# One load per side for a 576-row weight: 96 partitions of six rows instead of 128 partitions of four and a tail

## The chip, the cores and the metric

The kernel runs on one core of a Trainium2 chip. The metric is device time in microseconds (us) of one execution. The kernel before was timed in three runs: 249.95, 250.19 and 251.74 us, median 250.19 us. One execution was profiled; all durations below are from it.

## The reference, cut to what matters

Two independent decode steps of attention, A and B, each with one query token, 32 query heads, 16 key/value heads and a head size of 128. A attends to the last 2048 positions of its cache, B to all 8192. Everything is bf16.

```python
q = (x @ wq)                      # x: 1 x 576, wq: 576 x 4096  -> 32 heads of 128
k, v = k_cache[:, :, -W:], v_cache[:, :, -W:]   # W = 2048 (A), 8192 (B); 16 heads, each used twice
p = softmax(q @ k.T * 128**-0.5)
out = concat_heads(p @ v) @ wo    # wo: 4096 x 576
return concat([out_A, out_B])     # 1 x 1152
```

What has to be read from memory is wq and wo of both sides (4.72 MB each, four of them) and the caches (8 pairs of heads, each with 4.19 MB of B keys, 1.05 MB of A keys and the same of values).

## The kernel before, in words

**The ring.** All large loads go into one SBUF tensor, `ring`, of 73,728 bf16 elements on each of 128 partitions. `place` (L167) hands out consecutive stretches of it, starts again at 0 when a stretch doesn't fit, and makes the load wait for the last use of whatever its stretch overlaps. All loads are issued on SP in the order in which they are placed: wq of A, wq of B, then for each of 8 head pairs p the B keys, A keys, B values, A values, then wo of A in one piece and wo of B in six pieces. A load that waits holds up all loads behind it on SP. The two rows of x come over ACT's queue.

**wq before.** Of the 576 rows, 512 are loaded as 128 partitions of four rows (L197, 4.19 MB), the other 64 as 128 half rows (L199, 0.52 MB). In the ring, wq of A holds elements 0 to 18432, wq of B 18432 to 36864, the first keys and values follow, and the first B values (up to 73728) end exactly at the ring's end, so that the first seven loads wait for nothing.

**Spreading x.** The query is computed so that each of 128 output rows holds the same q: the stationary operand is a column of x repeated 128 times. `xT` (L272) makes these by five matmuls of a strided piece of x against ones; the fifth takes each of the last 64 elements twice, which `xd` (L263, VectorE) has written into `xdup` first. `xr` (L275, L278, VectorE) copies the results from PSUM to `xrep`; the fifth block is copied twice, each time multiplied by a 0/1 column `par` (L247) that keeps the even or the odd partitions, since an odd partition holds the second half of its row.

**q.** `qmm` (L295) makes q in eight pieces of 512 columns per side, five accumulating matmuls each. It waits for wq of its side and for all `xr` of both sides. ACT and VectorE take turns in evicting (`qe`), VectorE transposes (`qT`, L306) and scatters q into the zeroed stationary operands `zb` and `za` (`z0`, `z1`).

**The pairs.** For each head pair, VectorE transposes ten slabs of keys (`T`, L335), TensorE makes scores from each (`S`, L345), the maximum, the exponential and its transposes follow, and TensorE multiplies by the values (`V`, L393 and L400). `F` (L457) is the product with wo at the end, and two stores write the output. GpSimd builds identity and ones and clears `zb`, `za`, `pts` at the start (L229 to L241).

Of the kernel before, what the change touches and what calls it, by code (L numbers as in the profile page):

```python
# [4 lines left out]
BF16 = mybir.dt.bfloat16  # L5
F32 = mybir.dt.float32
I32 = mybir.dt.int32
ALU = mybir.AluOpType
ACT = mybir.ActivationFunctionType
AX = mybir.AxisListType  # L10
# [4 lines left out]
DM = 576  # L15
# [5 lines left out]
SLAB = 2048  # L21
NB = 2 * SK // 128 * DH // SLAB
NI = NB + 2
W0 = 2 * (NB - 1)
ZW = 128 + W0
RING = 72 * 1024
# [5 lines left out]
class Prog:  # L32
# [9 lines left out]
    def op(self, eng, fn, deps=(), name=None):  # L42
        self.ops[eng].append((fn, tuple(deps), name, None))
        if name is not None:
            assert name not in self.where, name
            self.where[name] = (eng, len(self.ops[eng]) - 1)
# [60 lines left out]
def bass_concat_heads__sliding_block_cached__gqa_block_cached__decode_kernel(nc, A_x, A_k_cache, A_v_cache, A_wq, A_wo,  # L107
                         B_x, B_k_cache, B_v_cache, B_wq, B_wo, out):
    xs, ks, vs = [A_x, B_x], [A_k_cache, B_k_cache], [A_v_cache, B_v_cache]
    wqs, wos = [A_wq, B_wq], [A_wo, B_wo]  # L110
# [7 lines left out]
    identf = nc.alloc_sbuf_tensor("identf", [128, 128], F32)  # L118
    onesf = nc.alloc_sbuf_tensor("onesf", [128, 128], F32)
    onesb = nc.alloc_sbuf_tensor("onesb", [1, 128], BF16)  # L120
    xrow = nc.alloc_sbuf_tensor("xrow", [1, 2 * DM], BF16)
    xdup = nc.alloc_sbuf_tensor("xdup", [1, 2, 128], BF16)
    xrep = nc.alloc_sbuf_tensor("xrep", [128, 2, 6, 128], BF16)
    qsb = nc.alloc_sbuf_tensor("qsb", [128, 2, 512], BF16)

# [10 lines left out]
    cls = nc.alloc_sbuf_tensor("cls", [128, 8], F32)  # L136
    selb = nc.alloc_sbuf_tensor("selb", [128, 16], F32)
    sela = nc.alloc_sbuf_tensor("sela", [128, 4], F32)
    par = nc.alloc_sbuf_tensor("par", [128, 2], F32)
    lsel = nc.alloc_sbuf_tensor("lsel", [128, NP, 8], F32)  # L140
    rl = nc.alloc_sbuf_tensor("rl", [128, NP * 8], F32)
    xo = nc.alloc_sbuf_tensor("xo", [128, 2, 512], F32)
# [12 lines left out]
    def view(t, free, offset, dims, parts=128, p0=0):  # L155
        return bass.AP(tensor=t, offset=p0 * free + offset, ap=[[free, parts], *dims])

    pg = Prog(nc)
    op, load = pg.op, pg.load
# [7 lines left out]
    def place(size, uses, issue, name):  # L167
        if at[0] + size > RING:
            at[0] = 0
        lo, hi = at[0], at[0] + size  # L170
        at[0] = hi
        deps = []
        for r in list(live):
            if r[0] < hi and lo < r[1]:
                deps += r[2]
                live.remove(r)
        n = nload[0]
        nload[0] += 1
        if n >= NSEM:
            deps += uses_of[n - NSEM]  # L180
        uses_of.append(list(uses))
        live.append((lo, hi, list(uses)))
        t = ring[:, lo:hi]
        load("sp", lambda e: issue(e, t), s_ld[n % NSEM], 16 * (n // NSEM + 1), deps=deps, name=name)
        return t

    for P in range(2):
        x = xs[P]
# [4 lines left out]
    wq_at = {}  # L193
    w = HQ * DH
    for P in range(2):
        uses = ["qmm%d.7" % P]
        main = wqs[P][0:512, :].rearrange("(p k) n -> p (k n)", k=4)  # L197
        wq_at[P, 0] = place(4 * w, uses, lambda e, t, main=main: e.dma_start(t, main), "wq%d.0" % P)
        tail = wqs[P][512:DM, :].rearrange("r (c n) -> (r c) n", c=2)  # L199
        wq_at[P, 1] = place(w // 2, uses, lambda e, t, tail=tail: e.dma_start(t, tail), "wq%d.1" % P)  # L200

    kv_at = {}
    for p in range(NP):
        for kind, c in (("K", ks), ("V", vs)):
            use = "T%d.%d" if kind == "K" else "V%d.%d"
            src = c[1][0, 2 * p:2 * p + 2, :, :].rearrange("h (q t) d -> (h q) (t d)", q=64)
            kv_at[kind, p, 0] = place(NB * SLAB, [use % (p, NB - 1)],
                                      lambda e, t, src=src: e.dma_start(t, src), "%sB%d" % (kind, p))
            src = c[0][0, 2 * p:2 * p + 2, SK - W_A:SK, :].rearrange("h (q t) d -> q h (t d)", q=128)
            kv_at[kind, p, 1] = place(2 * SLAB, [use % (p, NI - 1)],  # L210
                                      lambda e, t, src=src: e.dma_start(t.rearrange("q (h n) -> q h n", h=2), src),
# [3 lines left out]
    for P in range(2):  # L215
        k0 = 0
        for c, kk in enumerate(NWO[P]):
            src = wos[P].rearrange("(p k) n -> p (k n)", k=HQ)[:, k0 * DM:(k0 + kk) * DM]
# [4 lines left out]
    def slab(kind, p, s):  # L223
# [9 lines left out]
       deps=["id0"], name="ident")  # L233
# [9 lines left out]
    op("act", lambda e: e.activation(warm[:, 4:8], warm[:, 0:4], ACT.Exp), deps=["warm0"], name="warm1")  # L243
    for b in range(2):
        op("dve", lambda e, b=b: e.memset(vb[b][:, :], 0.0), name="vb0.%d" % b)
    for c in range(2):
        op("dve", lambda e, c=c: e.tensor_reduce(par[:, c:c + 1], view(identf, 128, c, [[2, 64]]), AX.X, ALU.add),  # L247
           deps=["identf"], name="par%d" % c)
    for h in range(2):
        op("dve", lambda e, h=h: e.tensor_reduce(  # L250
            cls[:, 2 * h:2 * h + 2], view(identf, 128, 64 * h, [[1, 2], [32, 2], [2, NB]]), AX.XY, ALU.add),
            deps=["identf"], name="clsB%d" % h)
    op("dve", lambda e: e.tensor_reduce(cls[:, 4:8], view(identf, 128, 2 * NB, [[1, 4], [32, 4]]), AX.X, ALU.add),
       deps=["identf"], name="clsA")
    op("dve", lambda e: e.tensor_reduce(selb[:], view(identf, 128, 0, [[1, 16], [32, 4]]), AX.X, ALU.add),
       deps=["identf"], name="selb")
    op("dve", lambda e: e.tensor_reduce(sela[:], view(identf, 128, 0, [[4, 2], [1, 2], [32, 4], [2, 2]]), AX.XY, ALU.add),
       deps=["identf"], name="sela")


    banks = [sb[0], sb[1], qb[0], qb[1]]
    for P in range(2):
        op("dve", lambda e, P=P: e.tensor_copy(  # L263
            view(xdup, 256, 128 * P, [[2, 64], [1, 2]], parts=1),
            view(xrow, 2 * DM, P * DM + 512, [[1, 64], [0, 2]], parts=1)), deps=["x%d" % P], name="xd%d" % P)
        for k in range(5):
            def mm(e, P=P, k=k):
                if k < 4:
                    lhsT = view(xrow, 2 * DM, P * DM + k, [[4, 128]], parts=1)
                else:  # L270
                    lhsT = xdup[0:1, P, :]
                return e.matmul(banks[2 * P + k // 4][:, (k % 4) * 128:(k % 4 + 1) * 128], lhsT=lhsT,  # L272
                                rhs=onesb[0:1, :], start=True, stop=True)
            op("pe", mm, deps=["x%d" % P, "onesb", "xd%d" % P], name="xT%d.%d" % (P, k))
        op("dve", lambda e, P=P: e.tensor_copy(  # L275
            xrep[:, P, 0:4, :].rearrange("p k m -> p (k m)"), banks[2 * P][:, :]), deps=["xT%d.3" % P], name="xr%d.0" % P)
        for c in range(2):
            op("dve", lambda e, P=P, c=c: e.tensor_scalar(  # L278
                xrep[:, P, 4 + c, :], banks[2 * P + 1][:, 0:128], par[:, c:c + 1], None, ALU.mult),
                deps=["xT%d.4" % P, "par%d" % c], name="xr%d.%d" % (P, 1 + c))  # L280
    XR = ["xr%d.%d" % (P, c) for P in range(2) for c in range(3)]

    KT = NKT * SLAB
    for P in range(2):
        for n in range(8):
            u = 8 * P + n
            bank = banks[u % 4]

            def mm(e, P=P, n=n, bank=bank):
                for k in range(5):  # L290
                    if k < 4:
                        lhsT, o = xrep[:, P, k, :], wq_at[P, 0][:, k * w + n * 512:k * w + (n + 1) * 512]
                    else:
                        lhsT, o = xrep[:, P, 4 + n // 4, :], wq_at[P, 1][:, (n % 4) * 512:(n % 4 + 1) * 512]
                    ins = e.matmul(bank[:, :], lhsT=lhsT, rhs=o, start=(k == 0), stop=(k == 4))  # L295
                return ins
            op("pe", mm, deps=["wq%d.0" % P, "wq%d.1" % P] + XR + (["qe%d" % (u - 4)] if u >= 4 else []),
               name="qmm%d.%d" % (P, n))
            deps = ["qmm%d.%d" % (P, n)] + (["qT%d" % (u - 2)] if u >= 2 else [])
            if n % 2 == 0:  # L300
                op("act", lambda e, n=n, bank=bank: e.activation(qsb[:, n % 2, :], bank[:, :], ACT.Copy),  # L301
                   deps=deps, name="qe%d" % u)
            else:
                op("dve", lambda e, n=n, bank=bank: e.tensor_copy(qsb[:, n % 2, :], bank[:, :]),
                   deps=deps, name="qe%d" % u)
            op("dve", lambda e, n=n: e.transpose(  # L306
                ktb[:, n * 512:(n + 1) * 512].bitcast(I32), qsb[:, n % 2, :].bitcast(I32)),
                deps=["qe%d" % u] + (["z0.%d" % i for i in range(8)] if P else []), name="qT%d" % u)
        srcs = [[512, NP], [64, 2], [1, 2], [128, 2]]
        for b in range(4):  # L310
            if P == 1:
                op("dve", lambda e, b=b: e.tensor_copy(
                    view(zb, NP * 4 * ZW, 32 * b + W0, [[4 * ZW, NP], [2 * ZW, 2], [ZW, 2], [1, 2]], 32, 32 * b),
                    view(ktb, KT, b // 2 * 256, srcs, 32, 32 * b)),
                    deps=["qT%d" % u for u in range(8, 16)] + ["zb0"], name="z1.%d" % b)
            else:
                for h in range(2):
                    op("dve", lambda e, b=b, h=h: e.tensor_copy(
                        view(za, NP * 1024, h * 512 + 32 * b + 2 * (NB + h),
                             [[1024, NP], [256, 2], [128, 2], [1, 2]], 32, 32 * b),  # L320
                        view(ktb, KT, h * 256, srcs, 32, 32 * b)),
                        deps=["qT%d" % u for u in range(8)] + ["za0"], name="z0.%d" % (2 * b + h))
# [6 lines left out]
    for p in range(NP):  # L329
        for s in range(NI):  # L330
            k = p * NI + s
            kt = ktb[:, (k % NKT) * SLAB:(k % NKT + 1) * SLAB]
            deps = [unit("K", p, s)]
            deps += ["S%d" % (k - NKT)] if k >= NKT else Z
            op("dve", lambda e, p=p, s=s, kt=kt: e.transpose(kt.bitcast(I32), slab("K", p, s).bitcast(I32)),  # L335
               deps=deps, name="T%d.%d" % (p, s))
# [12 lines left out]
            deps = ["T%d.%d" % (p, s)]  # L349
# [5 lines left out]
           deps=["S%d" % (p * NI + NI - 1)] + (["mT%d" % (p - 1)] if p else []), name="max%d" % p)  # L355
        op("pe", lambda e: e.matmul(mb[0:1, 0:128], lhsT=mx[:, 0:1], rhs=identf[:, :], start=True, stop=True),  # L356
           deps=["max%d" % p, "identf"] + (["mrA%d" % (p - 1), "mrB1.%d" % (p - 1), "nb%d" % (p - 1)] if p else []),
           name="mT%d" % p)
# [146 lines left out]
```

## Time and profile before

| | us |
|---|---|
| median of three runs | 250.19 |
| the profiled execution | 250.0 |
| its span, first to last instruction | 248.2 |
| TensorE matmul busy | 181.7 (73%) |
| VectorE busy | 153.1 (62%) |
| ScalarE busy | 18.1 |
| GpSimd busy | 13.4 |
| bytes read | 102.76 MB, 414 GB/s over the span |

"Busy" is time in which an engine has an instruction in execution, including one that is held up inside the engine. The time of the profiled execution is 1.8 us over its span: start and end around the instructions. The row of the DMA engines in the page gives the mean busy share of 16 engines in forty slices of 6.2 us; the row below it gives the rate. A load is listed with the time from its issue to the landing of its last byte, which includes the time that it queues behind the loads before it.

### The profile page before, as it was taken

Reading aid. Unit: us, or ns where it says so; the run is one execution under the profiler, and the core shown is the slowest. Engines: PE = TensorE matmul, PEld = TensorE weight load, DVE = VectorE, ACT = ScalarE, POOL = GpSimd, SP = SyncE. Lnnn points to the kernel's source line nnn. Section 1 sums busy time; section 2 is a strip of 40 time slices with the busy share of each in tenths; the row PEclk is TensorE's granted clock in tenths of the full one; section 3 lists DMA queues with packets and bytes.
Section 4 is the critical chain, followed back from the end, with each engine's and each line's share of the span. In section 5 each row is a group of like instructions: output and inputs, shape, how many; then the busy total and the mean of one; then the engine's idle time right before and its main releaser. Section 6 shows DMA issues by size and latency. Waiting matters only on the chain.

```text
span 248.2 us, 2581 instructions
## 1 busy us (share of the span) xinstructions
PE 181.7 (73%) x1085; PEld 80.7 (33%) x1085; DVE 153.1 (62%) x228; ACT 18.1 (7%) x36; POOL 13.4 (5%) x15
## 2 busy tenths in 40 slices
PE   0039994957995799379746984998489757975795
PEld 0013441313631342143224321732153124322552
DVE  8963779952885298439734873487349725972300
ACT  2001220010001000100010001000100010001000
POOL 8920000000000000000000000000000000000000
PEclk9999999795589599877987597569677957895769
DMA  7999999999999999999999999999999999999992
GB/s 264 418 490 433 422 422 416 417 428 418 427 414 434 419 458 419 436 432 431 421 429 414 434 422 428 420 422 419 433 420 433 428 433 422 436 403 457 395 406 111
DMA packets 8262, 102.92 MB, mean 415 GB/s; under 512 B 694, under 2 KB 956, under 8 KB 5564
## 3 DMA queue, kind: packets, MB, share of 16 engines
q1 hardware_dynamic: 8248, 102.77, 97.9%
q8 instruction: 8, 0.13, 0.2%
q14 instruction: 2, 0.02, 0.0%
q10 hardware_dynamic: 4, 0.00, 0.0%
HBM read 102.76 MB, written 0.00 MB: 414 GB/s over the span
## 4 chain that ended last, share of the span: by engine, by line
DMA 32%; DVE 31%; PE 30%; issue 3%; ACT 2%; SPq 0%; POOL 0%; POOLq 0%; DVEq 0%
DMA ring<-in_B_k_cache_dram 22%; DVE ktb L335 18%; DMA ring<-in_B_wo_dram 10%; PE sb L345 10%; PE vb L393 7%; DVE xdup L263 5%; PE sb L295 4%; PE qb L295 3%; DVE pts L384 3%; ACT psb L380 2%; PE ob L414 1%; DVE mx L354 1%; PE ob L421 1%; PE vb L400 1%; PE mb L356 1%
## 5 line engine op out<-in xcount | busy, mean ns | idle before, releaser
L335 DVE STREAM_TRANSPOSE ktb<-ring 128x1024 int32<-128x1024 int32 x80 | 92.4, 1213 | 11.3 <-DMA ring<-in_B_k_cache_dram 7.6
L345 PE MATMUL sb<-ktb,zb 128*128 128x512 bf16 x256 | 73.6, 443 | 11.0 <-DVE ktb L335 9.8
L345 PEld LDWEIGHTS sb<-ktb,zb 128*128 128x128 bf16 x256 | 25.6, 110 | 56.3 <-DVE ktb L335 24.2
L393 PE MATMUL vb<-ring,pts 128*16 128x512 bf16 x256 | 28.2, 619 | 21.1 <-DVE pts L384 21.1
L409 DVE COPY xo<-vb 128x512 f32<-128x512 f32 x8 | 5.5, 692 | 35.8 <-PE vb L400 35.8
L393 PEld LDWEIGHTS vb<-ring,pts 128*16 128x16 bf16 x256 | 8.5, 123 | 34.3 <-issue 34.2
L345 PE MATMUL sb<-ktb,za 128*128 128x512 bf16 x64 | 16.7, 381 | 1.3
L380 ACT ACTIVATE psb<-sb,nb 128x512 bf16<-128x512 f32 x8 | 5.5, 687 | 140.9 <-DVE nb L378 140.9
L384 DVE STREAM_TRANSPOSE pts<-psb 64x512 bf16<-64x512 bf16 x16 | 11.3, 706 | 7.0 <-ACT psb L380 6.8
L295 PE MATMUL sb<-ring,xrep 128*128 128x512 bf16 x40 | 11.2, 438 | 1.3 <-DVE xrep L278 1.3
L263 DVE COPY xdup<-xrow 1x128 bf16<-1x128 bf16 x2 | 11.3, 5660 | 0.0
L457 PE MATMUL qb<-ring,oP 128*1 128x288 bf16 x128 | 10.9, 346 | 0.5 <-DVE oP L446 0.4
L414 PEld LDWEIGHTS ob<-selb,xo 128*128 128x128 f32 x64 | 10.1, 242 | 3.4 <-ACT xo L407 3.4
L354 DVE TENSOR_REDUCE mx<-sb 128x1 f32<-128x512 f32 x8 | 5.5, 692 | 9.1 <-PE sb L345 9.1
L414 PE MATMUL ob<-selb,xo 128*128 128x4 f32 x64 | 10.8, 293 | 0.3 <-ACT xo L407 0.3
L272 PE MATMUL sb<-onesb,xrow 1*128 1x128 bf16 x4 | 0.6, 295 | 14.0 <-DVE xdup L263 14.0
L306 DVE STREAM_TRANSPOSE ktb<-qsb 128x256 int32<-128x256 int32 x16 | 7.0, 443 | 6.1 <-ACT qsb L301 5.8
L421 PE MATMUL ob<-sela,xo 128*128 128x2 f32 x64 | 9.9, 276 | 0.0
L421 PEld LDWEIGHTS ob<-sela,xo 128*128 128x128 f32 x64 | 9.5, 227 | 0.0
L295 PE MATMUL qb<-ring,xrep 128*128 128x512 bf16 x40 | 9.3, 379 | 0.0
L345 PEld LDWEIGHTS sb<-ktb,za 128*128 128x128 bf16 x64 | 4.9, 96 | 13.1 <-DVE ktb L335 9.2
L457 PEld LDWEIGHTS qb<-ring,oP 128*1 128x1 bf16 x128 | 6.1, 99 | 5.3 <-DMA ring<-in_B_wo_dram 1.2
(66 smaller groups left out, 83.0 us busy)
## 6 DMA issues: line engine op xcount, KB each, us to landing
ring<-in_B_k_cache_dram SPq DMA_DIRECT2D x8, 4096.0 KB, 27.0
ring<-in_B_v_cache_dram SPq DMA_DIRECT2D x8, 4096.0 KB, 26.8
ring<-in_A_k_cache_dram SPq DMA_DIRECT2D x8, 1024.0 KB, 28.9
ring<-in_A_v_cache_dram SPq DMA_DIRECT2D x8, 1024.0 KB, 27.2
ring<-in_A_wo_dram SPq DMA_DIRECT2D x1, 4608.0 KB, 28.2
ring<-in_A_wq_dram SPq DMA_DIRECT2D x1, 4096.0 KB, 12.2
ring<-in_B_wq_dram SPq DMA_DIRECT2D x1, 4096.0 KB, 22.3
ring<-in_B_wo_dram SPq DMA_DIRECT2D x1, 2304.0 KB, 33.4
```

What stands on the lines that cost most here:

```text
L263: op("dve", lambda e, P=P: e.tensor_copy(view(xdup, 256, 128 * P, [[2, 64], [1, 2]], parts=1), view(xrow, 2 * DM, P * DM + 512, [[1, 64], ...
L295: ins = e.matmul(bank[:, :], lhsT=lhsT, rhs=o, start=(k == 0), stop=(k == 4))
L306: op("dve", lambda e, n=n: e.transpose(ktb[:, n * 512:(n + 1) * 512].bitcast(I32), qsb[:, n % 2, :].bitcast(I32)), deps=["qe%d" % u] + ([" ...
L335: op("dve", lambda e, p=p, s=s, kt=kt: e.transpose(kt.bitcast(I32), slab("K", p, s).bitcast(I32)), deps=deps, name="T%d.%d" % (p, s))
L345: ins = e.matmul(sb[p % 2][:, :], lhsT=lhsT, rhs=view(ktb, KT, (k % NKT) * SLAB + 64 * c + v, [[128, 16], [2, 32]]), start=(s == 0 and c = ...
L354: op("dve", lambda e, p=p: e.tensor_reduce(mx[:, 0:1], sb[p % 2][:, :], AX.X, ALU.max), deps=["S%d" % (p * NI + NI - 1)] + (["mT%d" % (p - ...
L380: op("act", lambda e, p=p: e.activation(psb[:, :], sb[p % 2][:, :], ACT.Exp, bias=nb[:, p % 2:p % 2 + 1], scale=SCALE, accum_out=rsall[:, ...
L384: op("dve", lambda e, h=h: e.transpose(view(pts, 1024, 2 * h, [[4, 16], [64, 16], [1, 2]], 64, 64 * h), psb[64 * h:64 * h + 64, :]), deps= ...
L393: ins = e.matmul(vb[0][32 * j:32 * j + 16, :], lhsT=view(pts, 1024, 64 * s + 16 * j, [[1, 16]]), rhs=src[:, 512 * j:512 * j + 512], start= ...
L414: ins = e.matmul(ob[:, 8 * p:8 * p + 4], lhsT=xo[:, 0, 128 * t:128 * t + 128], rhs=selb[:, 4 * t:4 * t + 4], start=(t == 0), stop=(t == 3))
L421: ins = e.matmul(ob[:, 8 * p + 4 + 2 * h:8 * p + 6 + 2 * h], lhsT=xo[:, 1, 256 * h + 128 * t:256 * h + 128 * t + 128], rhs=sela[:, 2 * t:2 ...
L457: ins = e.matmul(fb[r:r + 1, 0:288], lhsT=oP[:, 1 - P, k0 + k:k0 + k + 1], rhs=wo_at[P, c][:, k * DM + 288 * n:k * DM + 288 * n + 288], st ...
```

## The change

The 576 rows of wq are taken as 96 partitions of six rows: one load per side, 49,152 bytes on each of 96 partitions, and the upper 32 partitions of that stretch of the ring stay unused. x is spread by six strided matmuls per side over 96 output partitions, and q is made by six accumulating matmuls over 96 partitions where there were five over 128. `xdup`, `xd`, `par` and the masked copies go; `xr` is two plain copies per side.

A stretch for wq is now 24,576 elements instead of 18,432, so all that is placed behind it moves. With the sizes of the code, the stretches and the first waits come out as follows (T0.7 is the transpose of the eighth slab of pair 0, and so on):

| load | before: stretch, waits for | after: stretch, waits for |
|---|---|---|
| wq A, wq B | 0 to 36864, nothing | 0 to 49152, nothing |
| first B keys | 36864 to 53248, nothing | 49152 to 65536, nothing |
| first A keys | 53248 to 57344, nothing | 65536 to 69632, nothing |
| first B values | 57344 to 73728, nothing | 0 to 16384, last q matmul of A |
| first A values | 0 to 4096, last q matmul of A | 16384 to 20480, the same |
| second B keys | 4096 to 20480, last q matmul of B | 20480 to 36864, last q matmul of B |
| second B values | 24576 to 40960, T0.7 | 40960 to 57344, T0.7 |
| third B keys | 45056 to 61440, V0.7 | 0 to 16384, V0.7 |
| wo of A | 40960 to 59392, V6.9 | 0 to 18432, V6.9 |
| wo of B, first two pieces | 59392 to 73216, long done | 18432 to 32256, T7.7 |
| wo of B, last four pieces | 0 to 4608, T7.7 | 32256 to 36864, T7.7 |

From the third pair of loads on, both kernels have the ring in three stretches of one B and one A load each, and each load waits for the use of the one three before it.

```diff
+KQ = 6
+PQ = DM // KQ
-        main = wqs[P][0:512, :].rearrange("(p k) n -> p (k n)", k=4)
-        wq_at[P, 0] = place(4 * w, uses, lambda e, t, main=main: e.dma_start(t, main), "wq%d.0" % P)
-        tail = wqs[P][512:DM, :].rearrange("r (c n) -> (r c) n", c=2)
-        wq_at[P, 1] = place(w // 2, uses, lambda e, t, tail=tail: e.dma_start(t, tail), "wq%d.1" % P)
+        src = wqs[P].rearrange("(p k) n -> p (k n)", k=KQ)
+        wq_at[P] = place(KQ * w, uses, lambda e, t, src=src: e.dma_start(t[0:PQ, :], src), "wq%d" % P)
...
-    for c in range(2):
-        op("dve", lambda e, c=c: e.tensor_reduce(par[:, c:c + 1], view(identf, 128, c, [[2, 64]]), AX.X, ALU.add),
-           deps=["identf"], name="par%d" % c)
...
-        op("dve", lambda e, P=P: e.tensor_copy(
-            view(xdup, 256, 128 * P, [[2, 64], [1, 2]], parts=1),
-            view(xrow, 2 * DM, P * DM + 512, [[1, 64], [0, 2]], parts=1)), deps=["x%d" % P], name="xd%d" % P)
-        for k in range(5):
-            def mm(e, P=P, k=k):
-                if k < 4:
-                    lhsT = view(xrow, 2 * DM, P * DM + k, [[4, 128]], parts=1)
-                else:
-                    lhsT = xdup[0:1, P, :]
...
+        for k in range(KQ):
+            op("pe", lambda e, P=P, k=k: e.matmul(
+                banks[2 * P + k // 4][0:PQ, (k % 4) * 128:(k % 4 + 1) * 128],
+                lhsT=view(xrow, 2 * DM, P * DM + k, [[KQ, PQ]], parts=1), rhs=onesb[0:1, :], start=True, stop=True),
+                deps=["x%d" % P, "onesb"], name="xT%d.%d" % (P, k))
         for c in range(2):
-            op("dve", lambda e, P=P, c=c: e.tensor_scalar(
-                xrep[:, P, 4 + c, :], banks[2 * P + 1][:, 0:128], par[:, c:c + 1], None, ALU.mult),
+            op("dve", lambda e, P=P, c=c: e.tensor_copy(
+                xrep[0:PQ, P, 4 * c:min(4 * c + 4, KQ), :].rearrange("p k m -> p (k m)"),
+                banks[2 * P + c][0:PQ, 0:128 * min(4, KQ - 4 * c)]),
...
-                for k in range(5):
-                    if k < 4:
-                        lhsT, o = xrep[:, P, k, :], wq_at[P, 0][:, k * w + n * 512:k * w + (n + 1) * 512]
-                    else:
-                        lhsT, o = xrep[:, P, 4 + n // 4, :], wq_at[P, 1][:, (n % 4) * 512:(n % 4 + 1) * 512]
-                    ins = e.matmul(bank[:, :], lhsT=lhsT, rhs=o, start=(k == 0), stop=(k == 4))
+                for k in range(KQ):
+                    ins = e.matmul(bank[:, :], lhsT=xrep[0:PQ, P, k, :],
+                                   rhs=wq_at[P][0:PQ, k * w + n * 512:k * w + (n + 1) * 512],
+                                   start=(k == 0), stop=(k == KQ - 1))
                 return ins
```

More of the change, by code (lines that the diff above doesn't have):

```diff
@@ L121, in bass_concat_heads__sliding_block_cached__gqa_block_cached__decode_kernel @@
     xrow = nc.alloc_sbuf_tensor("xrow", [1, 2 * DM], BF16)
-    xdup = nc.alloc_sbuf_tensor("xdup", [1, 2, 128], BF16)
     xrep = nc.alloc_sbuf_tensor("xrep", [128, 2, 6, 128], BF16)
@@ L138, in bass_concat_heads__sliding_block_cached__gqa_block_cached__decode_kernel @@
     sela = nc.alloc_sbuf_tensor("sela", [128, 4], F32)
-    par = nc.alloc_sbuf_tensor("par", [128, 2], F32)
     lsel = nc.alloc_sbuf_tensor("lsel", [128, NP, 8], F32)
@@ L262, in bass_concat_heads__sliding_block_cached__gqa_block_cached__decode_kernel @@
     for P in range(2):
-        op("dve", lambda e, P=P: e.tensor_copy(
-            view(xdup, 256, 128 * P, [[2, 64], [1, 2]], parts=1),
-            view(xrow, 2 * DM, P * DM + 512, [[1, 64], [0, 2]], parts=1)), deps=["x%d" % P], name="xd%d" % P)
-        for k in range(5):
-            def mm(e, P=P, k=k):
-                if k < 4:
-                    lhsT = view(xrow, 2 * DM, P * DM + k, [[4, 128]], parts=1)
-                else:
-                    lhsT = xdup[0:1, P, :]
[L272 to L276, printed above, removed]
-        for c in range(2):
-            op("dve", lambda e, P=P, c=c: e.tensor_scalar(
-                xrep[:, P, 4 + c, :], banks[2 * P + 1][:, 0:128], par[:, c:c + 1], None, ALU.mult),
-                deps=["xT%d.4" % P, "par%d" % c], name="xr%d.%d" % (P, 1 + c))
-    XR = ["xr%d.%d" % (P, c) for P in range(2) for c in range(3)]
+        for k in range(KQ):
[3 more added lines that the diff above has]
+                deps=["x%d" % P, "onesb"], name="xT%d.%d" % (P, k))
+        for c in range(2):
+            op("dve", lambda e, P=P, c=c: e.tensor_copy(
+                xrep[0:PQ, P, 4 * c:min(4 * c + 4, KQ), :].rearrange("p k m -> p (k m)"),
+                banks[2 * P + c][0:PQ, 0:128 * min(4, KQ - 4 * c)]),
+                deps=["xT%d.%d" % (P, min(4 * c + 4, KQ) - 1)], name="xr%d.%d" % (P, c))
+    XR = ["xr%d.%d" % (P, c) for P in range(2) for c in range(2)]
     KT = NKT * SLAB
@@ L289, in mm @@
             def mm(e, P=P, n=n, bank=bank):
-                for k in range(5):
-                    if k < 4:
-                        lhsT, o = xrep[:, P, k, :], wq_at[P, 0][:, k * w + n * 512:k * w + (n + 1) * 512]
-                    else:
-                        lhsT, o = xrep[:, P, 4 + n // 4, :], wq_at[P, 1][:, (n % 4) * 512:(n % 4 + 1) * 512]
-                    ins = e.matmul(bank[:, :], lhsT=lhsT, rhs=o, start=(k == 0), stop=(k == 4))
+                for k in range(KQ):
+                    ins = e.matmul(bank[:, :], lhsT=xrep[0:PQ, P, k, :],
+                                   rhs=wq_at[P][0:PQ, k * w + n * 512:k * w + (n + 1) * 512],
+                                   start=(k == 0), stop=(k == KQ - 1))
                 return ins
-            op("pe", mm, deps=["wq%d.0" % P, "wq%d.1" % P] + XR + (["qe%d" % (u - 4)] if u >= 4 else []),
+            op("pe", mm, deps=["wq%d" % P] + XR + (["qe%d" % (u - 4)] if u >= 4 else []),
                name="qmm%d.%d" % (P, n))
```

## The prediction

> **What bounds the kernel now.** I read the row of the DMA engines first, since this kernel reads 102.76 MB once. Page, parts 2 and 3:
>
> ```profile
> DMA  7999999999999999999999999999999999999992
> GB/s 264 418 490 433 422 422 416 417 428 418 427 414 434 419 458 419 436 432 431 421 429 414 434 422 428 420 422 419 433 420 433 428 433 422 436 403 457 395 406 111
> q1 hardware_dynamic: 8248, 102.77, 97.9%
> ```
>
> The DMA engines are busy from the second slice to the last but one: no slice in which a load came too late. So the end is the sum of all bytes over the engines' rate, and a wait on a compute engine costs nothing until it leaves the load queue empty. The rate at the place of the change comes from the loads issued in the first 30 us (KB each, us from issue to landing), with SP's issues in order of time (start, duration):
>
> ```profile
> ring<-in_A_wq_dram SPq DMA_DIRECT2D x1, 4096.0 KB, 12.2
> ring<-in_B_wq_dram SPq DMA_DIRECT2D x1, 4096.0 KB, 22.3
> ring<-in_B_k_cache_dram SPq DMA_DIRECT2D x1, 4096.0 KB, 32.2
> ring<-in_B_v_cache_dram SPq DMA_DIRECT2D x1, 4096.0 KB, 45.0
> ...
> ring<-in_A_wq_dram SPq DMA_DIRECT2D x1, 512.0 KB, 13.0
> ring<-in_B_wq_dram SPq DMA_DIRECT2D x1, 512.0 KB, 23.1
> ```
>
> ```profile
> 0.74 0.39 SPq L198 DMA_DIRECT2D ring<-in_A_wq_dram  x1
> 1.19 0.41 SPq L200 DMA_DIRECT2D ring<-in_A_wq_dram  x1
> 1.65 0.43 SPq L198 DMA_DIRECT2D ring<-in_B_wq_dram  x1
> 2.12 0.53 SPq L200 DMA_DIRECT2D ring<-in_B_wq_dram  x1
> 2.69 0.44 SPq L208 DMA_DIRECT2D ring<-in_B_k_cache_dram  x1
> ...
> 28.89 0.38 SPq L211 DMA_DIRECT2D ring<-in_A_v_cache_dram  x1
> 37.52 0.33 SPq L208 DMA_DIRECT2D ring<-in_B_k_cache_dram  x1
> ```
>
> The large parts of wq land at 0.74+12.2=12.94 and 1.65+22.3=23.95: 11.0 us for one large part and one tail, 4.72 MB, or 429 GB/s. The first B keys land at 2.69+32.2=34.9, again 10.9 us per 4.72 MB. By the same addition the tails land at 14.2 and 25.2. The trace's packet records give the same rate per engine: 128 packets per large load, 8 on each of 16 engines, 1.213 us for one of 32,768 bytes, 27.0 GB/s. They are as long in the first pair as in the last.
>
> Then the chain of waits, because it names another suspect (start, us, what):
>
> ```profile
> 2.86 11.04 DVE xdup L263
> ...
> 18.10 4.28 PE sb L295 x10
> ...
> 35.33 1.09 PE qb L295 x5
> ...
> 39.70 6.90 DVE ktb L335 x6
> ...
> 219.43 25.99 DMA ring<-in_B_wo_dram
> ```
>
> An 11 us copy of one row stands at its head, and looks like 11 us to be had. It isn't: at its end, 13.90, the tail of wq A (14.2) hasn't landed either, and the end of the chain is a DMA, the last piece of wo, landing at 245.42. The copies `T` of the keys wait for loads in places too (7.6 us in five waits in the table of groups), so compute has caught up with the loads by the later pairs.
>
> **The change, part by part.** The profiled execution took 250.0 us, 248.2 of them its span, 0.2 below the median of 250.19; I add to the median.
>
> *Spreading x.* Gone are two `par` (0.35 us), `xd` (11.04 and 0.13) and four masked copies (0.60 per side); new are one matmul per side (five take 0.60, so 0.12 more) and a copy of 256 columns (half of the 512-column copy of 0.69, some 0.35). VectorE's 11 us end with GpSimd's run of memsets (busy to 14.2; the second `xd` takes 0.20), so it was held, not working. Whether the new copies from PSUM are held as well no row shows: if not, `xr` is ready by some 6 us, if so by 13.9 plus 2 x (0.69+0.35), 16.0. wq A isn't there before 14.2, so the difference is 1.8 us at most, and behind it stands wq B at 25.2.
>
> *q.* 96 matmuls for 80, of 512 columns as before. Ten took 4.28 us at first and ten 2.16 after that, so 0.216 us each and sixteen more 3.5 us. For A: ten slow and 38 fast, 12.5 us, from 14.2 (or 16.0) to 26.7 (or 28.5), where it is 28.9 now. For B: 48 x 0.216 = 10.4, from 26.7 (28.5) to 37.1 (38.9), now 37.5. The extra matmuls eat what the earlier start gives: between 0.4 earlier and 1.4 later, and the load queue hides both.
>
> *The ring.* The first B values now wait for the last q matmul of A, 26.7 to 28.5 instead of 3.67, with everything behind them on SP. What is queued without a wait is 14.7 MB, at 429 GB/s until 1.3+34.2=35.5 us: 7 us of cover. The second B keys wait for the last q matmul of B as before, with 5.2 MB more ahead of them, to 47.7: 8.8 us or more of cover. Later waits keep their partner, some moved by two slabs (2.4 us of transposes, under 1 us of matmuls), against loads that land 27 us after issue, of which 12 are for one B and one A load: 15 us of cover. The first two pieces of wo B now wait for T7.7, at 218.1 instead of 206.8; wo A lands at 206.06+28.2=234.3, so 16 us of cover. Without its cover each would cost its delay less what is queued. Here, nothing.
>
> *The load itself.* The bytes stay (96 x 49,152 is 4.72 MB). The trace shows no large load on fewer than 128 partitions, so I bound it. Lower end: if only bytes per engine count and 96 partitions spread evenly, six packets at 27.0 GB/s are the 11.0 us of now; the two tails' short packets save 16 x 7 ns an engine, 0.1 us (159 ns for 4,096 bytes against 152 at the long packets' rate). Less than that would need engines over the 27.0 GB/s that no long packet exceeds. Next: if the rate goes with partitions (429 GB/s over 128 is 3.35 per partition; or, with the same result, the eight packets to an engine stay eight and twelve engines work), a side takes 11.0 x 128/96 = 14.7 us, 3.7 more. Upper end: engines get into each other's way for all of the load and run at half rate, 11.0 more per side. I take the middle, as its row is nearest: the large loads of the trace are all laid out as eight rows to an engine, and their rate is all that it shows.
>
> A side's 3.7 us isn't made up later. Each engine works its own queue at 27.0 GB/s without a break. The packet records show it: the last of the 16 engines ends a load 0.5 us after the first in the first three loads, 1.95 us at 48 us, and still 2.4 us at 230 us. An engine that falls 7.3 us behind in the first 30 us is 7.3 us behind with the last piece of wo.
>
> [...]
>
> Sum: 2 x 3.7 = 7.3 us; 250.2 + 7.3 = **257.5 us**, 2.9% slower. Compute stays inside it: wq B lands at 1.3+29.3=30.6, q of B ends at 41 to 43, so the first T starts 3.5 to 5.5 us later than at 39.70, less than the loads' 7.3.
>
> **The rivals.**
>
> 1. *No loss.* The split is even and nothing else limits: 250.1 us, no change. For it: one long packet goes at 27.0 GB/s to one partition, so a partition isn't what limits. It decides if no packet of 49,152 bytes takes longer than 1.82 us and each engine gets six.
> 2. *Engines block each other.* [...] Half rate throughout is 2 x 11.0 = 22: 272.2. Between this and the forecast lie part collisions, 261 to 272. [...]
> 3. *The ring runs dry.* If q of A ends after 35.5 us, SP's wait empties the queue, and each us later costs one. It takes 7 us of delay where I find at most 1.8; if wq were late by that much, the queue would be late by it too.
> 4. *Faster.* The 11 us at the head of the chain come off: 239. Against it stand the full DMA row and wq's landing at 14.2. Compute can start 0.4 us earlier at best.
>
> **How the numbers follow.** Forecast (254 to 261): 0.48. No loss (249.5 to 252): 0.20. Blocking (261 to 273): 0.28. Ring dry: 0.02, priced with the forecast's upper part. Faster: 0.02. The range runs from the no-loss case at 249.6 to 269, most of the way to rival 2's end, which leaves out some 0.1 at the top and the faster case; the unknown price alone makes it that wide. One per cent, 2.5 us, is about what can be told from no change. Faster 0.02, same 0.20, slower 0.78.
>
> **What the profile after would show.** The load of wq A landing some 16 us after the start and that of B some 31, where the parts land at 14.2 and 25.2 now; the first B keys at 42 instead of 34.9. The first five slices near 320 GB/s, all later slices as now, at a DMA row without holes. q of A starting within 1 us of the landing of wq A; `xdup` gone without a trace in the end. If wq B lands by 25 and the time is still longer, I am wrong about the load, and the issue times of the first B values and second B keys say whether the ring ran dry. If it lands after 35, it is blocking.

## The result and the profile after

The changed kernel takes 272.66 us (median of 4 runs, 272.05 to 273.74) against 250.07 us beside it: 1.089 times as long, 95% interval 1.083 to 1.095, or 22.6 us more. The forecast was 257.5 us with a range to 269; the time lies above it, at the price of the second rival (272.2). The profiled execution took 272.75 us, its span 271.0.

The page of the changed kernel, parts 2 and 3 (forty slices of 6.8 us):

```profile
DMA  9997998999999999999999999999999999999993
GB/s 232 218 203 160 232 232 194 435 408 447 402 409 442 403 446 443 408 440 409 455 397 460 383 470 379 472 389 460 411 437 414 418 443 394 455 412 453 400 412 116
HBM read 102.76 MB, written 0.00 MB: 379 GB/s over the span
```

The row of the DMA engines is as full as before; what changed is the rate under it. For seven slices, 47 us, the engines move 160 to 232 GB/s, then 379 to 472 up to the last slice, where before it was 395 to 490 between the first slice and the last. In this row a packet counts as busy for as long as it takes: below, the share is 1.13 at 238 GB/s and 1.01 at 420. So the row alone can't tell a slow transfer from a fast one.

The same stretch of the changed kernel's trace in stages of 6.2 us (after the stage: its length, busy time and count of TensorE, its weight loads, VectorE, ScalarE and GpSimd, then TensorE's granted clock, the DMA share and GB/s):

```profile
0.00:6.20 6.20, 1.06 (x6) 0.87 (x6) 2.61 (x9) 1.49 (x2) 5.42 (x11) 1.00 1.10 238
...
18.60:24.80 6.20, 0.00 (x0) 0.00 (x0) 0.00 (x0) 0.00 (x0) 0.00 (x0) 1.00 1.13 238
...
49.60:55.80 6.20, 6.20 (x24) 2.55 (x23) 2.11 (x5) 1.19 (x2) 0.00 (x0) 0.77 0.99 428
55.80:62.00 6.20, 5.06 (x24) 2.08 (x22) 4.15 (x8) 1.19 (x2) 0.00 (x0) 1.00 1.01 420
```

From 18.6 to 24.8 us no compute engine does anything: all wait for wq of A. The stages say where the loss ends as well: behind the last byte of wq, which lands at 48.3 us, the rate is 428 and 420.

The loads issued in the first 60 us of the changed kernel (KB, us from issue to landing), and SP's issues (start, duration):

```profile
ring<-in_A_wq_dram SPq DMA_DIRECT2D x1, 4608.0 KB, 25.1
ring<-in_B_wq_dram SPq DMA_DIRECT2D x1, 4608.0 KB, 47.1
ring<-in_B_k_cache_dram SPq DMA_DIRECT2D x1, 4096.0 KB, 57.7
```

```profile
0.74 0.39 SPq L198 DMA_DIRECT2D ring<-in_A_wq_dram  x1
1.19 0.40 SPq L198 DMA_DIRECT2D ring<-in_B_wq_dram  x1
1.63 0.43 SPq L206 DMA_DIRECT2D ring<-in_B_k_cache_dram  x1
2.11 0.76 SPq L209 DMA_DIRECT2D ring<-in_A_k_cache_dram  x1
39.44 0.35 SPq L206 DMA_DIRECT2D ring<-in_B_v_cache_dram  x1
```

wq of A lands at 0.74+25.1=25.8 us (its tail landed at 14.2 before), wq of B at 48.3 (25.2 before). Between the two landings lie 22.4 us for 4.72 MB, 210 GB/s, where it was 429. The packet records of the trace put it per packet: 192 of 49,152 bytes, sixteen under way at a time, so six behind one another for each load, with a median of 3.7 us where 27.0 GB/s would be 1.82; half of them took between 3.60 and 3.83 us, none less than 2.78 or more than 4.22. So both loads run at about half rate from the first packet to the last, in all sixteen chains of packets alike (their sixteen landings lie between 24.7 and 25.8 us for A, 47.0 and 48.3 for B). The first B values, issued late at 39.44, find the first B keys still on their way (1.63+57.7=59.3): the queue did not run dry. The chain of waits of the changed kernel, at its end, is again a DMA:

```profile
242.96 25.20 DMA ring<-in_B_wo_dram
268.16 0.04 issue
268.20 0.31 PE qb L442 x2
```

It lands at 268.2, 22.7 us after the 245.4 of before. That is the delay of wq of B (23.1) but for 0.4.

### The profile page after: what moved, and what is told of

Read it like the earlier page. It is cut to its first block, busy times and chain, and to the rows that moved or that the text cites. A ratio compares the mean times of both kernels' runs of the same rounds, so it can differ in the third digit from the quotient of the medians.

```text
span 271.0 us, 2603 instructions
## 1 busy us (share of the span) xinstructions
PE 186.6 (69%) x1103; PEld 81.8 (30%) x1103; DVE 141.4 (52%) x222; ACT 18.1 (7%) x36; POOL 13.4 (5%) x15
## 4 chain that ended last, share of the span: by engine, by line
DMA 56%; PE 20%; DVE 18%; issue 2%; ACT 1%; SPq 1%; DVEq 0%
DMA ring<-in_B_k_cache_dram 30%; DMA ring<-in_B_wq_dram 17%; DVE ktb L320 13%; DMA ring<-in_B_wo_dram 9%; PE sb L330 8%; PE vb L378 5%; PE sb L278 3%; DVE pts L369 2%; PE qb L278 2%; ACT psb L365 1%; DVE mx L339 1%; SPq L217 1%; PE mb L361 1%; PE mb L341 1%; DVE mr L346 0%
## 5 line engine op out<-in xcount | busy, mean ns | idle before, releaser
L330 PEld LDWEIGHTS sb<-ktb,zb 128*128 128x128 bf16 x256 | 25.3, 109 | 57.1 <-DVE ktb L320 25.8
L278 PE MATMUL sb<-ring,xrep 96*128 96x512 bf16 x48 | 15.6, 493 | 19.7 <-DMA ring<-in_A_wq_dram 10.8
L330 PE MATMUL sb<-ktb,za 128*128 128x512 bf16 x64 | 16.7, 381 | 1.3
L278 PEld LDWEIGHTS sb<-ring,xrep 96*128 96x128 bf16 x48 | 5.5, 119 | 28.7 <-DMA ring<-in_A_wq_dram 11.0
L278 PE MATMUL qb<-ring,xrep 96*128 96x512 bf16 x48 | 11.5, 391 | 0.0
L442 PE MATMUL qb<-ring,oP 128*1 128x288 bf16 x128 | 9.9, 317 | 1.4 <-DMA ring<-in_B_wo_dram 0.9
L406 PE MATMUL ob<-sela,xo 128*128 128x2 f32 x64 | 9.1, 264 | 0.0
L406 PEld LDWEIGHTS ob<-sela,xo 128*128 128x128 f32 x64 | 8.6, 210 | 0.0
L259 PE MATMUL qb<-onesb,xrow 1*96 1x128 bf16 x6 | 1.1, 342 | 10.7 <-DMA xrow<-in_B_x_dram 10.7
L385 PE MATMUL vb<-ring,pts 128*8 128x256 bf16 x128 | 7.7, 385 | 0.0
## 6 DMA issues: line engine op xcount, KB each, us to landing
ring<-in_A_wq_dram SPq DMA_DIRECT2D x1, 4608.0 KB, 25.1
```

The source lines that it names most:

```text
L278: ins = e.matmul(bank[:, :], lhsT=xrep[0:PQ, P, k, :], rhs=wq_at[P][0:PQ, k * w + n * 512:k * w + (n + 1) * 512], start=(k == 0), stop=(k ...
L330: ins = e.matmul(sb[p % 2][:, :], lhsT=lhsT, rhs=view(ktb, KT, (k % NKT) * SLAB + 64 * c + v, [[128, 16], [2, 32]]), start=(s == 0 and c = ...
L385: ins = e.matmul(vb[1][32 * j:32 * j + 8, 256 * h:256 * h + 256], lhsT=view(pts, 1024, 64 * s + 8 * t, [[1, 8]]), rhs=src[:, 256 * t:256 * ...
L406: ins = e.matmul(ob[:, 8 * p + 4 + 2 * h:8 * p + 6 + 2 * h], lhsT=xo[:, 1, 256 * h + 128 * t:256 * h + 128 * t + 128], rhs=sela[:, 2 * t:2 ...
L442: ins = e.matmul(fb[r:r + 1, 0:288], lhsT=oP[:, 1 - P, k0 + k:k0 + k + 1], rhs=wo_at[P, c][:, k * DM + 288 * n:k * DM + 288 * n + 288], st ...
```

## Experiments

**Packet length or partitions.** The two things that 49,152 bytes on 96 partitions have in common with no load of the kernel before are the length of the piece and the number of partitions. The first run keeps the partitions and changes the length:

```diff
-        src = wqs[P].rearrange("(p k) n -> p (k n)", k=KQ)
-        wq_at[P] = place(KQ * w, uses, lambda e, t, src=src: e.dma_start(t[0:PQ, :], src), "wq%d" % P)
+        src = wqs[P].rearrange("(k p) n -> p k n", k=KQ)
+        wq_at[P] = place(KQ * w, uses, lambda e, t, src=src: e.dma_start(
+            t[0:PQ, :].rearrange("p (k n) -> p k n", k=KQ), src), "wq%d" % P)
...
-                lhsT=view(xrow, 2 * DM, P * DM + k, [[KQ, PQ]], parts=1), rhs=onesb[0:1, :], start=True, stop=True),
+                lhsT=view(xrow, 2 * DM, P * DM + k * PQ, [[1, PQ]], parts=1), rhs=onesb[0:1, :], start=True, stop=True),
```

> The changed kernel with one thing different: row 96k+p instead of 6p+k goes to partition p, so the same 96 partitions get six pieces of 8,192 bytes each in place of one of 49,152, and x is spread to match. In the changed kernel each of the 192 packets of 49,152 bytes took 3.6 to 3.8 us, twice the 1.82 us of 27.0 GB/s. [...] Theory 2, the length of the packet (49,152 bytes, where the longest one at full rate was 36,864): wq of A lands near 13 us and of B near 24, total 250 us.

Measured: 272.71 us, 1.088 times before (1.084 to 1.093). The row of rates on its page:

```profile
GB/s 156 210 213 211 212 212 249 397 442 408 451 402 455 381 464 381 476 388 462 402 450 407 416 434 408 459 414 440 426 427 424 401 456 397 453 416 440 414 408 145
```

The same 210 GB/s with pieces a sixth as long, and with the rows dealt to the partitions in another order. Neither the length of the piece (theory 2) nor that order makes the loss. (Not every packet of the changed kernel took the 3.6 to 3.8 us that the expectation names: they took 2.78 to 4.22.)

**The load's shape alone.** The second run leaves everything else of the change in place and spreads the same bytes over all partitions; q is then made from the wrong parts of wq:

```diff
-        src = wqs[P].rearrange("(p k) n -> p (k n)", k=KQ)
-        wq_at[P] = place(KQ * w, uses, lambda e, t, src=src: e.dma_start(t[0:PQ, :], src), "wq%d" % P)
+        src = wqs[P].rearrange("r (c n) -> (r c) n", c=2).rearrange("(p k) n -> p (k n)", k=9)
+        wq_at[P] = place(KQ * w, uses, lambda e, t, src=src: e.dma_start(t[:, 0:9 * w // 2], src), "wq%d" % P)
...
-                                   rhs=wq_at[P][0:PQ, k * w + n * 512:k * w + (n + 1) * 512],
+                                   rhs=wq_at[P][0:PQ, (8 * k + n) % 36 * 512:((8 * k + n) % 36 + 1) * 512],
```

> The changed kernel with its ring, its waits, its six matmuls over 96 partitions and its one load per side, but the load lays the same 4.72 MB out as 36,864 contiguous bytes on each of 128 partitions. It makes q from the wrong parts of wq. Theory 1, the set of partitions: wq of A lands near 12.5 us, of B near 23.5, total 250 us (249.5 to 251). Theory 3, the waits and places that moved in the ring, the six matmuls or the spreading of x cost the 22.6 us: 272 us stays. Anything between is their share.

Measured: 250.11 us, 0.9997 times before (0.997 to 1.0025). Its loads:

```profile
ring<-in_A_wq_dram SPq DMA_DIRECT2D x1, 4608.0 KB, 13.6
ring<-in_B_wq_dram SPq DMA_DIRECT2D x1, 4608.0 KB, 24.0
```

They land at 0.74+13.6=14.3 and 1.18+24.0=25.2 us, as the tails did before (14.2 and 25.2); the 12.5 and 23.5 of the expectation were too early. All 22.6 us go with the shape of the load. The rest of the change, with its six matmuls, its two plain copies, its one load instead of two and all its moved waits, comes to nothing. In particular the 11 us copy that stood at the head of the chain of waits is gone here too, and not a microsecond comes of it.

**The ring alone.** The kernel before with the ring places of the changed one:

```diff
-        wq_at[P, 1] = place(w // 2, uses, lambda e, t, tail=tail: e.dma_start(t, tail), "wq%d.1" % P)
+        wq_at[P, 1] = place(2 * w, uses, lambda e, t, tail=tail: e.dma_start(t[:, 0:w // 2], tail), "wq%d.1" % P)
```

> The kernel before with its two loads per side and its spreading of x, but 24,576 elements of the ring set aside for each wq, so that all later loads have the places and the waits of the changed kernel. Theory 1: 250.2 us, within 0.5, since the first B values issued at 28.9 instead of 3.7 us still find 7 us of queued loads. Theory 3, the ring: up to 272 us; the ring alone can cost only what SP's first B values come after 35.5 us.

Measured: 249.97 us, 1.0004 times before (0.997 to 1.004). Its trace has the first B values issued at 28.83 us; the queued loads cover it, as the prediction had worked out.

**The cost by itself.** One kernel, called the ladder below, with fifteen loads from the B keys, each issued when the one before has landed (the lines below the first few differ only in partitions, length and semaphore):

```python
eng.dma_start(ring[0:128, 0:16384], rows(128, 32)).then_inc(sems[0], 16)
eng.wait_ge(sems[0], 16)
...
eng.dma_start(ring[32:128, 0:16384], rows(96, 32)).then_inc(sems[5], 16)
eng.wait_ge(sems[5], 16)
```

> The cost by itself: fifteen loads from the B keys, each issued when the one before has landed, nothing else but a store of zeros as output (no attention is computed). 32,768 bytes on each partition unless said; 128 rows at 27.0 GB/s on each of 16 engines are 9.7 us, with some 2.5 us of start and landing (12.2 us for the first load of the kernel before). [...] A share per partition: 12 us for all with 32,768 bytes. Theory 2, packet length: 128 rows of 49,152 bytes 32 us and 96 rows of 32,768 bytes 10 us. 112, 120, 80 and 48 rows are open.

SP's issues in its trace. The time from one start to the next is the time of the first of the two loads:

```profile
0.73 0.39 SPq L130 DMA_DIRECT2D ring<-in_B_k_cache_dram  x1
12.94 0.34 SPq L132 DMA_DIRECT2D ring<-in_B_k_cache_dram  x1
25.08 0.33 SPq L134 DMA_DIRECT2D ring<-in_B_k_cache_dram  x1
42.15 0.34 SPq L136 DMA_DIRECT2D ring<-in_B_k_cache_dram  x1
66.59 0.32 SPq L138 DMA_DIRECT2D ring<-in_B_k_cache_dram  x1
83.28 0.31 SPq L140 DMA_DIRECT2D ring<-in_B_k_cache_dram  x1
100.04 0.31 SPq L142 DMA_DIRECT2D ring<-in_B_k_cache_dram  x1
116.63 0.54 SPq L144 DMA_DIRECT2D ring<-in_B_k_cache_dram  x1
129.29 0.54 SPq L146 DMA_DIRECT2D ring<-in_B_k_cache_dram  x1
136.85 0.33 SPq L148 DMA_DIRECT2D ring<-in_B_k_cache_dram  x1
144.08 0.32 SPq L150 DMA_DIRECT2D ring<-in_B_k_cache_dram  x1
161.12 0.38 SPq L152 DMA_DIRECT2D ring<-in_B_k_cache_dram  x1
183.30 0.32 SPq L154 DMA_DIRECT2D ring<-in_B_k_cache_dram  x1
197.46 0.31 SPq L156 DMA_DIRECT2D ring<-in_B_k_cache_dram  x1
211.69 0.35 SPq L158 DMA_DIRECT2D ring<-in_B_k_cache_dram  x1
223.85 0.26 SPq L161 DMA_DIRECT2D out_dram<-outsb  x1
```

A load of 128 rows of 32,768 bytes takes 12.2 us (its two repeats, L132 and L158, 12.14 and 12.16), of which 9.7 are the bytes at 27.0 GB/s per engine; the other 2.5 are put down to start and landing and taken off below for all. All lines are from one execution, and each shape but the first stands in it once:

| line | partitions | bytes on each | us | GB/s without 2.5 us |
|---|---|---|---|---|
| L130 | 0 to 127 | 32,768 | 12.21 | 432 |
| L134 | 0 to 127 | 49,152 | 17.07 | 432 |
| L136 | 0 to 95 | 49,152 | 24.44 | 215 |
| L138 | 0 to 95 | 32,768 | 16.69 | 222 |
| L140 | 32 to 127 | 32,768 | 16.76 | 221 |
| L142 | 16 to 111 | 32,768 | 16.59 | 223 |
| L144 | 0 to 63 | 32,768 | 12.66 | 206 |
| L146 | 32 to 95 | 32,768 | 7.56 | 414 |
| L148 | 0 to 31 | 32,768 | 7.23 | 222 |
| L150 | 0 to 111 | 32,768 | 17.04 | 252 |
| L152 | 0 to 119 | 32,768 | 22.18 | 200 |
| L154 | 0 to 79 | 32,768 | 14.16 | 225 |
| L156 | 0 to 47 | 32,768 | 14.23 | 134 |

Three things are to be seen. First, 96 rows take longer than 128: 16.7 us for three quarters of the bytes of 12.2. The rate doesn't go with the number of partitions, which was the forecast's step. Nor does it go with the length of the piece: 128 rows of 49,152 bytes run at 432 GB/s. Second, 64 rows are slow from partition 0 (206 GB/s) and fast from partition 32 (414), with the same bytes from the same place in memory, in as many packets, sixteen of them at a time: which partitions they go to decides, not how many. Third, 96 rows are slow from each of the three starts: 222 GB/s from 0, 221 from 32, 223 from 16. Neither case of the expectation passes: a share per partition would make 12 us of all rows of 32,768 bytes (7.23 to 22.18 were measured), the length of the packet 32 us of 128 rows of 49,152 bytes (17.07) and 10 us of 96 rows (16.69). The trace doesn't name the engine of a packet, and why the rate hangs on the rows in this way no run shows.

**The same partitions, loaded in two pieces.** This tests, with a case not in the ladder, whether the division of each load by itself sets its rate; which rows go to which engine it can't tell. The changed kernel again, each load cut at partition 32:

```diff
-        wq_at[P] = place(KQ * w, uses, lambda e, t, src=src: e.dma_start(t[0:PQ, :], src), "wq%d" % P)
+        wq_at[P] = place(KQ * w, uses, lambda e, t, src=src: e.dma_start(t[0:32, :], src[0:32, :]), "wq%d" % P)
+        load("sp", lambda e, P=P, src=src: e.dma_start(wq_at[P][32:PQ, :], src[32:PQ, :]), s_wq[P], 16, name="wr%d" % P)
...
-            op("pe", mm, deps=["wq%d" % P] + XR + (["qe%d" % (u - 4)] if u >= 4 else []),
+            op("pe", mm, deps=["wq%d" % P, "wr%d" % P] + XR + (["qe%d" % (u - 4)] if u >= 4 else []),
```

> The changed kernel with the same 96 partitions, packets of 49,152 bytes, ring and matmuls, but each side's load issued as two, partitions 0 to 31 and 32 to 95. In the ladder 32 rows from 0 ran at half rate and 64 rows from 32 at full rate. Theory 1, in the form that a load's own division over the engines decides which of them meet: two packets per engine at 3.64 us and four at 1.82 are 14.6 us per side, 3.6 more than before, wq of A lands near 17 us and of B near 31, total 257.4 us. Rival: 96 partitions are slow however they are loaded: 272.7 us. Rival: one load per side was the fault and two or more are free of it: 250.1 us.

Measured: 258.24 us, 1.033 times before (1.029 to 1.037). Its loads in the first 31 us:

```profile
ring<-in_A_wq_dram SPq DMA_DIRECT2D x1, 3072.0 KB, 18.0
ring<-in_B_wq_dram SPq DMA_DIRECT2D x1, 3072.0 KB, 31.4
ring<-in_A_wq_dram SPq DMA_DIRECT2D x1, 1536.0 KB, 10.7
ring<-in_B_wq_dram SPq DMA_DIRECT2D x1, 1536.0 KB, 25.1
```

The 257.4 of the expectation lies inside the interval (257.2 to 259.2 us), and both rivals are out. wq itself is complete at 1.19+18.0=19.2 and 2.55+31.4=34.0 us, later than the expected 17 and 31. One instruction more per side gives back 14.4 of the 22.6 us, on the same 96 partitions with the same packets. In its packet records 98 of the 192 packets take 2.2 us or less, 49 more than 3.6, and 45 stand between; the expectation had 128 short and 64 long ones. Why some stand between no run shows.

**A small dose.** The kernel before with its last 64 rows on partitions 0 to 63. Their stretch of the ring is twice as long, so the later loads move here too, and the first B values are issued at 29.55 us instead of 3.67; the run with the new places alone, at 28.83, lost nothing by that:

```diff
-        tail = wqs[P][512:DM, :].rearrange("r (c n) -> (r c) n", c=2)
-        wq_at[P, 1] = place(w // 2, uses, lambda e, t, tail=tail: e.dma_start(t, tail), "wq%d.1" % P)
+        tail = wqs[P][512:DM, :]
+        wq_at[P, 1] = place(w, uses, lambda e, t, tail=tail: e.dma_start(t[0:64, :], tail), "wq%d.1" % P)
...
-                    lhsT = view(xrow, 2 * DM, P * DM + k, [[4, 128]], parts=1)
+                    lhsT, m = view(xrow, 2 * DM, P * DM + k, [[4, 128]], parts=1), 128
                 else:
-                    lhsT = xdup[0:1, P, :]
+                    lhsT, m = view(xrow, 2 * DM, P * DM + 512, [[1, 64]], parts=1), 64
...
-                        lhsT, o = xrep[:, P, 4 + n // 4, :], wq_at[P, 1][:, (n % 4) * 512:(n % 4 + 1) * 512]
+                        lhsT, o = xrep[0:64, P, 4, :], wq_at[P, 1][0:64, n * 512:(n + 1) * 512]
```

> The kernel before, but the last 64 rows of wq go whole, 8,192 bytes each, to partitions 0 to 63 instead of as 128 half rows to 128 partitions; the doubling of x and the masks go with it. In the ladder 64 rows from partition 0 ran at half rate. Theory 1, that the rate of a load hangs on its partitions alone, small loads included: four packets on each engine at twice 0.31 us are 2.4 us where eight of 0.159 took 1.3, so 1.2 us more per side and 2.3 in all: 252.4 us. Rival: only long loads lose, or a loss this short is made up by the loads behind it: 250.1 us.

Measured: 253.47 us, 1.0144 times before (1.0108 to 1.0181), 3.5 us where 2.3 were expected. Half a megabyte per side is enough to be seen at the end of 250 us, and nothing behind it makes it up. The tails:

```profile
ring<-in_A_wq_dram SPq DMA_DIRECT2D x1, 512.0 KB, 15.2
ring<-in_B_wq_dram SPq DMA_DIRECT2D x1, 512.0 KB, 26.4
```

They land at 1.18+15.2=16.4 and 2.46+26.4=28.9, 2.2 and 3.7 us later than before. The median packet of the tails took 0.61 us, near the twice 0.31 of the expectation. The excess over the expected 2.3 us lies in packets of 32,768 bytes: 55 of them took more than 1.3 us, where the kernel before has 19, most of these at the very start. Over the usual 1.22 us they add 2.4 us on each of sixteen engines in the mean, before 0.7. What made them slow isn't in the trace.

None of the versions is faster than the kernel before. The one with the full spread equals it.

## Why the prediction was wrong

**What bounds the kernel: right.** It is the DMA engines: a version without the 11 us copy, with moved waits and sixteen more matmuls runs in 250.1 us.

**Spreading x: right in what it costs, but neither of its two cases came.** The first copies from PSUM ran beside GpSimd's memsets and weren't held (timeline of the changed kernel; the GpSimd line is the memset of `zb`):

```profile
1.89 3.88 POOL L234 MEMSET zb<- 128x4544 bf16 x1
3.18 1.02 DVE L264 CAST xrep<-sb 96x512 bf16<-96x512 f32 x2 [0.57 <-PE sb L259]
14.07 1.05 PE L259 MATMUL qb<-onesb,xrow 1*96 1x128 bf16 x6 [10.66 <-DMA xrow<-in_B_x_dram]
14.90 1.02 DVE L264 CAST xrep<-qb 96x512 bf16<-96x512 f32 x2 [10.70 <-PE qb L259]
```

The other side's came at 14.90 all the same, because its x landed late, at 14.0 us. `xr` was ready at 15.9, near the 16.0 of the worse of the two cases, by another cause, and it was hidden either way. The "some 6 us" of the better case left out that landing: in the kernel before it is at 7.8 us.

**q: the right size.** 25.90 to 39.4 us for A and 48.3 to 60.9 for B, 13.5 and 12.6 us against 12.5 and 10.4 to 12.5 (10.4 in the working of q, 12.5 in the sum): B's first twelve matmuls were slow too, 4.79 us, where each later twelve took 2.75.

**The ring: right**, shown by the run with the new places alone.

**The load: the step that failed.** The prediction bounded a side's extra at 0, 3.7 and 11.0 us and took 3.7, "if the rate goes with partitions". Measured is the upper end, 11.4: 22.4 us for a side instead of 11.0. The reason given for the choice was that the row of 128 partitions is the nearest; but a kernel with loads of 128 partitions alone can't tell a rate that goes with partitions from one that goes with where they lie. Nor is it a part of the load that loses, the case between the forecast and the second rival: 96 rows from 32 or from 16 (221 and 223 GB/s) lose as much as from 0 (222), and in the changed kernel no packet took less than 2.78 us, where 27.0 GB/s would be 1.82. Why 96 rows lose half stays open. The run with 32 and 64 rows in separate loads comes out near the forecast (258.2 us), but by accident: its 14.8 us from wq of A to wq of B, about three quarters of the rate of before, are the price of that division, not of the one that the load got.

**Not made up: right, and it carries the result.** The delay of wq of B at 48 us, 23.1, is 22.7 at the last load.

**The rivals.** No loss fell with the first look at the loads. The ring didn't run dry. Faster was excluded for the reason given. Of blocking, the prediction's own sign came (wq of B landing after 35 us: 48.3) and the price worked out for it (272.2 against 272.66). That engines block each other no run shows; what the runs show is the half rate that the price was worked out from, 210 GB/s instead of 429. This rival had 0.28 where the forecast had 0.48, and the range ended 3.2 us below its price.

## What to carry to other kernels

In a kernel that its loads bound, look at the destination of every load before its count of bytes: 96 rows cost more than 128, in these runs twice the time per byte (222 against 432 GB/s), and the same load cut in two at partition 32 gave back 14.4 of the 22.6 us. Bytes laid out over all 128 partitions were worth the masked copies and the odd tail here: 250.07 against 272.66 us. Where no row of the profile has the shape that a change introduces, the nearest row is no measure of it; fifteen loads in a row measure it in one run.

## What the runs showed of the hardware that was not expected

- A DMA row at nine tenths and a half rate go together: a packet that takes twice as long counts as busy for all of it (47 us of the changed kernel at 160 to 232 GB/s).
- 120 rows were the slowest of all for their bytes but 48: 22.2 us for 3.93 MB. Its packets stand in fifteen chains of eight in the records, and each took 2.5 us. 112 rows gave 252 GB/s, 48 rows 134; why these two differ from half rate stays open.
- In the changed kernel the second row of x, 1,152 bytes on ACT's queue, was issued at 1.27 us, and its reader could start at 14.07; the first, issued at 0.73, had its reader started at 2.35. wq's packets had begun to move on SP's queue at 1.8 us. The packet of the second row took 0.1 us itself, but started at 9.2 us, and its landing is recorded at 14.0. It landed at 7.8 us in the kernel before, 7.2 with 36,864 bytes on 128 partitions, 8.5 with the pieces of 8,192 bytes and 11.1 with the load in two, so it was latest where wq's packets were long and slow.
